# Turned score blocks in another layout, and the feed-forward part put under the list plan

## The chip, the core and the metric

The kernel runs on one core of a Trainium2 chip. The metric is device time in microseconds. TensorE (PE) multiplies, with its weight loads (PEld) beside it; VectorE (DVE) and ScalarE (ACT) do all elementwise work; SyncE (SP) issues nearly all DMAs.

## What is computed

Two batches of 3008 tokens. Attention without softmax, then two feed-forward networks (FFNs), all in float32:

```python
scores = scale * np.matmul(z, z.transpose(0, 2, 1))      # z: 2 x 3008 x 64
attn = np.maximum(scores, 0.0) ** 2
x = u * np.matmul(attn, v)                               # u, v: 2 x 3008 x 256
h = np.maximum(x @ moe_w_in, 0.0)                        # 256 -> 2048
x = h * h @ moe_w_out                                    # 2048 -> 256
h = x @ moe2_w_in
y = (h - np.tanh(h)) @ moe2_w_out
```

The weights come in float64, as pairs of 32-bit words.

## The kernel before

**Precision.** Each operand of a product is split into a high part (rounded to fp32r) and a low part, and each product is three matmuls: high by high, low by high, high by low. The splits are DVE and ACT work: an ACT copy or DVE cast makes the high part, a DVE subtraction the low part.

**Attention.** The queries of a batch are cut into six chunks (five of 512, the last of 448), so there are chunks 0 to 11. In each chunk 12 steps go over pairs of key blocks (256 keys). A step has scores (`scores`, L551, six matmuls of 64 rows), `relu` (L507) and `square` (L518) on ACT, `cast` to the high part (L487 on ACT or L489 on DVE), `low` (L496, DVE) and `values` (L588, 24 matmuls of 64 rows, two row groups at a time) that add into four PSUM banks. At the chunk's end `take` (L603 on ACT, L605 on DVE) evacuates the banks; the next chunk's values wait for it. `gate` (L610, DVE) multiplies with u for the first EARLY = 4 chunks, and `keep` stores x in DRAM; for the later chunks that product is made in the FFN part (`split_x`, L281).

**Mirrored steps.** The score matrix is symmetric. A pair of keys that lies in an earlier chunk is not computed again: `put` (L440) stores the squared block in DRAM, `get` (L446) loads it, `turn` (L456, or L462 twice in the last chunk of a batch) transposes its 32x32 blocks on DVE, and `cast` and `low` follow. In chunk t of a batch (t from 0 to 5) 2t of the 12 steps are mirrored: 60 in all. To make this fit, `keys` (L419) reads the keys of the first ten pairs in steps of four columns, `load_v` (L149) loads the rows of v in the same order, and relu writes runs of 128 (`views`, `wide`).

**Weights.** Each of the 32 weight units (16 a network, 512 KB after the split) costs nine operations in `split_w`: L240, L241, L244, L247 on the raw words, L250 and L253 on DVE, L242, L243 and L252 on ACT. 24 units are split during attention: STAY = 6 stay on chip, KEEP0 + KEEP1 = 18 are stored in DRAM and fetched at the end of attention. The last 8 are loaded and split in the FFN.

**Order.** In attention a planner writes the order of each engine: `attend` makes a Job for each operation with a cost, a due time (key), what it waits for and which buffers it takes and gives; `drive` plays them on a model of the engines (`ready`, `best`, `room`) and emits each in the order in which the model starts it. A turn costs 1.25 us there, or 1.4 (L1027). Weight units are due between step 10 and the start of chunk 5 in batch 0, and between step 76 and the start of chunk 11 in batch 1 (L954, L955). In the FFN the order is a fixed pattern: `front` (L643, six matmuls, then the elementwise work) runs LOOK = 3 steps ahead of `back` (L711, six matmuls); `interleave`, `pace`, `fill` and the lanes spread the weight and x splits between them. The steps of the first FFN (m1) run 21 steps ahead of those of the second (m2), one of each in turn.

Of the kernel before, what the change touches and what calls it, by code (L numbers as in the profile page):

```python
# [24 lines left out]
MARGIN = 6  # L25
READY = 3
# [17 lines left out]
def kernel(  # L44
# [221 lines left out]
    def load_x(c):  # L266
# [7 lines left out]
        return x, u

    def split_x(c, raw):
        n = chunks[c][2]
# [9 lines left out]
    class Lane:  # L287

        def __init__(self, units, ahead, width):
            self.todo, self.loaded, self.active = deque(units), deque(), deque()
            self.ahead, self.width = ahead, width

        def load(self, n, ready):
            need, _, load, split, args, nops = self.todo.popleft()
            self.loaded.append((need, ready, split, args, load(*args), nops))  # L300

        def refill(self, n, due):
            while (
                self.todo
                and len(self.loaded) + len(self.active) < self.ahead
                and self.todo[0][1] <= n
            ):
                self.load(n, n + READY)
            while self.loaded and len(self.active) < self.width:
                need, ready, split, args, raw, _ = self.loaded[0]  # L310
                if need > n if due else ready > n:
                    return
                self.loaded.popleft()
                self.active.append((need, deque(split(*args, raw)), n))

        def head(self):
            return min((u[0] for q in (self.active, self.loaded) for u in q), default=1 << 30)

        def pop(self, n, due, kinds):

            self.refill(n, due)
            if due:
                assert self.active or self.loaded or not self.todo or self.todo[0][0] > n
            for unit in self.active:


                if unit[0] <= n if due else unit[2] <= n and unit[1][0][0] in kinds:
# [870 lines left out]
```

## Time and profile before

| what | value |
|---|---|
| median of 3 runs (lowest to highest) | 1500.78 us (1499.35 to 1501.24) |
| profiled execution | 1500.66 us |
| its span | 1498.8 us |
| PE busy | 1481.7 us (99%), 8512 matmuls |
| DVE busy | 1262.8 us (84%) |
| ACT busy | 1048.9 us (70%) |
| mean granted clock of PE | 0.998 |

The span runs from the first instruction to the last. Busy matmuls reach into the time behind them, so a full PE row doesn't say that PE runs at its full rate; matmuls counted over a stretch do. Attention's first value matmul starts at 8.69 us, the FFN's first matmul at 467.01 us.

### The profile page before, as it was taken

Reading aid. Unit: us, or ns where it says so; the run is one execution under the profiler, and the core shown is the slowest. Engines: PE = TensorE matmul, PEld = TensorE weight load, DVE = VectorE, ACT = ScalarE, POOL = GpSimd, SP = SyncE. Lnnn points to the kernel's source line nnn. Section 1 sums busy time; section 2 is a strip of 40 time slices with the busy share of each in tenths; the row PEclk is TensorE's granted clock in tenths of the full one; section 3 lists DMA queues with packets and bytes.
Section 4 is the critical chain, followed back from the end, with each engine's and each line's share of the span. In section 5 each row is a group of like instructions: output and inputs, shape, how many; then the busy total and the mean of one; then the engine's idle time right before and its main releaser. Section 6 shows DMA issues by size and latency. Waiting matters only on the chain.

```text
span 1498.8 us, 22087 instructions
## 1 busy us (share of the span) xinstructions
PE 1481.7 (99%) x8512; PEld 1252.5 (84%) x8512; DVE 1262.8 (84%) x1907; ACT 1048.9 (70%) x1662; POOL 0.3 (0%) x6
## 2 busy tenths in 40 slices
PE   9999999999999999999999999999999999999999
PEld 7898878888878888888888888888888888888888
DVE  7899999888996899778788888878778787878788
ACT  8987558887654777667666666667666666766688
POOL 0000000000000000000000000000000000000000
PEclk9999999999999999999999999999999999999999
DMA  8857656777757200101001010101001010000000
GB/s 244 273 189 274 215 190 200 262 250 238 250 209 258 95 29 0 43 1 39 1 1 42 1 42 1 42 1 40 2 1 43 0 39 1 15 0 1 15 1 27
DMA packets 71529, 134.06 MB, mean 89 GB/s; under 512 B 4992, under 2 KB 47360, under 8 KB 67584
## 3 DMA queue, kind: packets, MB, share of 16 engines
q1 hardware_dynamic: 71120, 132.29, 25.9%
q8 instruction: 66, 1.08, 0.3%
q10 hardware_dynamic: 304, 0.38, 0.1%
q14 instruction: 39, 0.32, 0.1%
HBM read 79.43 MB, written 53.22 MB: 89 GB/s over the span
## 4 chain that ended last, share of the span: by engine, by line
PE 84%; DVE 10%; DMA 2%; ACT 2%; issue 2%; SPq 0%; DVEq 0%; ACTq 0%
PE o L711 34%; PE s L643 34%; PE o L588 14%; DVE at L456 3%; PE s L551 3%; DVE l L496 2%; DVE at L462 2%; ACT h L487 1%; DMA wraw<-in_moe_w_out_dram 1%; DMA zraw<-in_z_dram 1%; DMA wd<-wk 0%; DVE e L605 0%; DMA ww<-wd 0%; DVE wk L253 0%; DMA vraw<-in_v_dram 0%
## 5 line engine op out<-in xcount | busy, mean ns | idle before, releaser
L711 PE MATMUL o<-h,ww 128*128 128x512 f32 (+1 forms) x2304 | 576.2, 385 | 0.2 <-DVE h L658 0.2
L643 PE MATMUL s<-xs,ww 128*128 128x512 f32 (+1 forms) x2304 | 575.2, 385 | 0.0
L711 PEld LDWEIGHTS o<-h,ww 128*128 128x128 f32 x2304 | 432.4, 188 | 82.3 <-DVE h L658 0.7
L643 PEld LDWEIGHTS s<-xs,ww 128*128 128x128 f32 x2304 | 432.5, 188 | 81.1 <-issue 0.3
L588 PE MATMUL o<-h,vw 64*128 64x512 f32 (+1 forms) x2256 | 380.4, 387 | 5.2 <-DVE e L605 2.8
L588 PEld LDWEIGHTS o<-h,vw 64*128 64x128 f32 x2256 | 280.9, 186 | 44.1 <-DVE e L605 6.3
L588 PE MATMUL o<-l,vw 64*128 64x512 f32 (+1 forms) x1128 | 296.5, 387 | 6.9 <-DVE l L496 6.8
L658 DVE TENSOR_TENSOR h<-a,h 128x512 fp32r<-128x512 f32 (+1 forms) x192 | 130.7, 681 | 123.7 <-ACT h L656 122.7
L651 ACT ACTIVATE a<-s 128x512 f32<-128x512 f32 (+1 forms) x192 | 113.0, 589 | 173.2 <-PE s L643 171.4
L670 ACT ACTIVATE f<-s 128x512 f32<-128x512 f32 (+1 forms) x192 | 114.8, 598 | 125.9 <-PE s L643 125.9
L588 PEld LDWEIGHTS o<-l,vw 64*128 64x128 f32 x1128 | 172.1, 186 | 29.4 <-DVE l L496 10.9
L673 DVE TENSOR_TENSOR a<-s,a 128x512 f32<-128x512 f32 (+1 forms) x192 | 130.3, 678 | 32.9 <-ACT a L671 21.4
L689 DVE COPY_PREDICATED a<-small,f 128x512 f32<-128x512 uint8 (+1 forms) x171 | 127.3, 744 | 5.5
L487 ACT ACTIVATE h<-at 128x1024 fp32r<-128x1024 f32 (+1 forms) x60 | 61.5, 1024 | 93.2 <-DVE at L456 36.4
L652 ACT ACTIVATE a<-a 128x512 f32<-128x512 f32 (+1 forms) x192 | 119.7, 623 | 6.1
L692 DVE TENSOR_TENSOR h<-a,h 128x512 fp32r<-128x512 f32 (+1 forms) x172 | 117.9, 685 | 5.9
L686 DVE TENSOR_TENSOR f<-s,f 128x512 f32<-128x512 f32 (+1 forms) x171 | 117.2, 685 | 5.8
L672 ACT ACTIVATE f<-f 128x512 f32<-128x512 f32 (+1 forms) x192 | 121.7, 634 | 0.0
L671 ACT ACTIVATE a<-s 128x512 f32<-128x512 f32 (+1 forms) x192 | 113.9, 593 | 0.0
L656 ACT ACTIVATE h<-a 128x512 fp32r<-128x512 f32 (+1 forms) x171 | 106.4, 622 | 5.5
L496 DVE TENSOR_TENSOR l<-a,h 128x1024 fp32r<-128x1024 f32 (+1 forms) x83 | 100.2, 1208 | 10.4 <-ACT h L487 10.0
L518 ACT ACTIVATE a<-a 128x1024 f32<-128x1024 f32 (+1 forms) x83 | 87.1, 1052 | 1.2
(63 smaller groups left out, 1081.5 us busy)
## 6 DMA issues: line engine op xcount, KB each, us to landing
ad<-a SPq DMA_DIRECT2D x60, 512.0 KB, 4.2
m<-ad SPq DMA_DIRECT2D x30, 1024.0 KB, 6.5
wd<-wk SPq DMA_DIRECT2D x18, 512.0 KB, 3.0
ww<-wd SPq DMA_DIRECT2D x18, 512.0 KB, 7.7
wraw<-in_moe_w_in_dram SPq DMA_DIRECT2D x32, 256.0 KB, 4.8
wraw<-in_moe_w_out_dram SPq DMA_DIRECT2D x32, 256.0 KB, 4.9
vraw<-in_v_dram SPq DMA_DIRECT2D x22, 256.0 KB, 4.0
xr<-xd SPq DMA_DIRECT2D x10, 512.0 KB, 3.4
```

What stands on the lines that cost most here:

```text
L496: V.tensor_sub(l_, a_, h_)
L588: T.matmul(o[r * KD + d][:, :n], lhsT=w[halves[r], hl, g * D + d * P : g * D + (d + 1) * P], rhs=mv[halves[r], g, :n], start=x == 0 and (r ...
L643: T.matmul(s_, lhsT=w[:, hl, kd * P : (kd + 1) * P], rhs=mv[:, kd, :n], start=j == 0, stop=j == len(seq) - 1,)
L652: A.activation(a_, a_, AF.Square)
L658: main.append(lambda: V.tensor_sub(l[:, :n], a_, h[:, :n]))
L670: A.activation(f_, s_, AF.Tanh, scale=TB)
L672: A.activation(f_, f_, AF.Square, scale=TC)
L673: main = [lambda: V.tensor_sub(a_, s_, a_)]
L686: main.append(lambda: V.tensor_mul(g_, s_, f_))
L689: late.append(lambda: V.copy_predicated(a_, mask, g_))
L692: late.append(lambda: V.tensor_sub(l[:, :n], a_, h[:, :n]))
L711: T.matmul(o[d][:, :n], lhsT=w[:, side, (KD + d) * P : (KD + d + 1) * P], rhs=mv, start=k == 0 and j == 0, stop=k == NF - 1 and j == len(t ...
```

## The change

- `turn` is one DVE transpose for every chunk; it reads runs of 32 elements and writes in steps of four elements (16 bytes). The blocks in `put` and `get` keep their DMAs, but relu, cast, low and the opening now walk the score tiles in runs of 32 (`wide`, `views`, `cut`).
- `keys` and `load_v` take natural blocks of 128 keys and rows for every pair; still one DMA loads a pair of v blocks.
- The FFN's steps become Jobs of the same planner (`forward`); `front` and `back` keep their matmuls, and their elementwise work falls apart into `bend`, `power`, `shape`, `shape2`, `differ`, `mask`, `times`, `pick`, `high` and `rest`. `high` may go to ACT or DVE. The lanes and the fixed pattern are gone.
- m1 runs 41 steps ahead of m2, and this shrinks to 21 between m2's steps 32 and 160.
- 16 units are split in attention in place of 24 (KEEP0 + KEEP1 = 10); they are due one chunk earlier. The other 16 are split in the FFN.
- EARLY is 1: the product with u moves into the FFN for chunks 1 to 3.
- The planner counts buffers anew (w, h, raw, a, small, f, o), lets raw loads and h tiles take a free w buffer, counts two DMA issues for loads that send two, and looks only 60 us ahead.

The core of the diff:

```diff
-STAY, KEEP0, KEEP1 = 6, 6, 12
+STAY, KEEP0, KEEP1 = 6, 2, 8
 LANES = 8
-EARLY = 4
+AHEAD = 60.0
+EARLY = 1
...
-    lead = NF + LAG
+    lead = 2 * NF + LAG + 4
     steps += m1[:lead]
+    given = lead
     for i in range(len(m2)):
         steps.append(m2[i])
-        if lead + i < len(m1):
-            steps.append(m1[lead + i])
+        ahead = lead - (NF + 4) * min(max(i - 2 * NF, 0), 8 * NF) // (8 * NF)
+        while given < min(len(m1), i + 1 + ahead):
+            steps.append(m1[given])
+            given += 1
...
-            if j < 2 * (NC - 1):
-                rows = v[b, j // 2 * NMAX : (j // 2 + 1) * NMAX, :]
-                rows = rows.rearrange("(p t k) d -> t p k d", p=P, t=2)[j % 2]
-            else:
-                rows = v[b, 2 * j * P : 2 * (j + 1) * P, :].rearrange("(k p) d -> p k d", p=P)
+            rows = v[b, 2 * j * P : 2 * (j + 1) * P, :].rearrange("(k p) d -> p k d", p=P)
...
-        if p < 2 * (NC - 1):
-            return z.rearrange("r (p t k) -> r t k p", t=2, k=2)[:, p % 2, g]
...
-        if c % NC < NC - 1:
-            V.transpose(
-                a.rearrange("p g (j k) -> p k g j", k=16),
-                m.rearrange("p k (i t g) -> t p k g i", t=2, g=2)[p % 2],
-            )
-        else:
-            for g in range(2):
-                V.transpose(
-                    a[:, g].rearrange("p (s j m) -> p m s j", s=4, m=4),
-                    m.rearrange("p (m s) (i t g) -> t g p m s i", m=4, t=2, g=2)[p % 2, g],
-                )
+        V.transpose(
+            a.rearrange("p g (k j m) -> p m k g j", k=4, m=4),
+            m.rearrange("p (m k) (t g i) -> t p m k g i", m=4, t=2, g=2)[p % 2],
+        )
 
     def wide(x):
-        return x.rearrange("p (a x) -> p a x", a=4)
+        return x.rearrange("p (k a i) -> p k a i", k=4, a=4)
...
-            a.rearrange("p a g x -> p g a x"),
-            *(y.rearrange("p g (a x) -> p g a x", a=4) for y in tiles),
+            a.rearrange("p a g (k i) -> p g k a i", k=4),
+            *(y.rearrange("p g (k a i) -> p g k a i", k=4, a=4) for y in tiles),
...
+    def cut(a, g):
+        return a[:, :, g].rearrange("p a (k i) -> p k a i", k=4)
 
...
+        s = got[i] = single["s"].tile([P, NMAX], F32, tag="s", name="s")
...
+    def bend(i, func):
+
+        n = chunks[steps[i][1]][2]
+        a = sq[i] = ap_.tile([P, NMAX], F32, tag="a", name="a")[:, :n]
+        A.activation(a, got[i][:, :n], func)
+
+    def power(i):
+        A.activation(sq[i], sq[i], AF.Square)
...
+    def high(i, e, pool):
+
+        n = chunks[steps[i][1]][2]
+        pair[i] = pool.tile([P, 2, NMAX], F32R, tag="h" if pool is hp else "w", name="h")[:, :, :n]
+        if e == "A":
+            A.activation(pair[i][:, 0], sq[i], AF.Copy)
+        else:
+            V.tensor_copy(pair[i][:, 0], sq[i])
+
+    def rest(i):
+        V.tensor_sub(pair[i][:, 1], sq[i], pair[i][:, 0])
...
-        "w": [0.0] * (NW - 6),
-        "h": [0.0, 3.0],
+        "w": [0.0] * (NW - 6) + [4.0, 8.0],
+        "h": [0.0],
...
+    spare = {"h": 0, "raw": 2}
+    owed = [0]
...
+    def choices(pool):
+
+        if pool in spare and len(room["w"]) > owed[0] + spare[pool]:
+            times = room["w"][: len(room["w"]) - owed[0] - spare[pool]]
+            return sorted(room[pool] + times)
+        return room[pool]
...
+            if found and job.key > max(reached[0], found[0][1].key) + AHEAD:
+                break
...
+        ahead = at["m1", 0, 0]
+        for n in range(ahead, len(steps)):
+            until = min(n + (LOOK if n < end else FAR), len(steps) - 1)
+            while ahead <= until:
+                order_p.append(("f", ahead))
+                ahead += 1
+            order_p.append(("b", n))
...
+            hi = (b + 1) * nv - 2 * NV
+            if k < split:
+                step = lo + (k - first + 1) * (hi - lo) // count
+                need, asks = when["o", step], max(step - 12, 6)
+            else:
+                t0, t1 = when["f", at["m1", 0, 0]], when["f", at["m2", 0, 0]]
+                need = t0 + 6.0 + (k - split + 1) * (t1 - t0 + 10.0) / (2 * NF - split)
+                need, asks = min(need, when["f", at["m2", 0, f]] - 4.0), at["att", NCH - 1, 0] + 10
...
+                wjob[m, f] = Job(
+                    bring,
+                    when["f", at["m1", 0, f]] - 12.0,
+                    [(last + min(kept + 2, NV - 1), 0.0), (stages[-1], 0.0)],
+                    ["w"],
+                    S=2.6,
+                )
...
+            X = [("A", 1.06), ("V", 0.69), ("V", 0.69)]
+            give = [(2, xs_)]
+            if c >= EARLY:
+                X = [("V", 1.23), *X]
+                give = [(3, xs_), (0, us_)]
+                after.append((Job(ask2, need - 16.0, [(asks, 0.0)], ["raw"], [us_], S=2.6), 0.0))
...
+    def forward(kind, c, k, when, size, wjob, whold, xjob, xhold):
+
+        i = at[kind, c, k]
+        m, f = int(kind == "m2"), size(i)
+        alone = i > at["m1", NCH - 1, NF - 1]
+        need = when["b", i]
+        part = 1.36 if f == 1 else 1.22
+        s_, a, t_, small, hs = hold("f"), hold("a"), hold("t"), hold("z" if alone else "small"), hold(None)
+        after = [(wjob[m, k], 0.0), *xjob[m, c]]
+        if i == at["m1", 0, 0]:
+            after.append((("relu", NCH - 1), 0.0))
+        go = Job(lambda e, pools: front(i), when["f", i], after, ["f"], [xhold[m, c]], P=part)
+        go.name = ("f", i, 0)
+        A6, A63, V42, V69 = 0.6 * f, 0.63 * f, 0.42 * f, 0.69 * f
+        if m == 0:
+            one = Job(lambda e, pools: bend(i, AF.Relu), need - 3.2, [(go, 0.0)], ["a"], [s_], A=A6)
+            one = Job(lambda e, pools: power(i), need - 2.5, [(one, 0.0)], (), (), A=A63)
...
+        hi = Job(
+            lambda e, pools: high(i, e, homes[pools[0]]), need - 1.8, [(one, 0.0)], ["h"], [hs], A=A63, V=V42
+        )
+        lo = Job(lambda e, pools: rest(i), need - 0.8, [(hi, 0.0)], (), [a], V=V69)
+        give = [hs] + ([whold[m, k]] if c == NCH - 1 else [])
+        after = [(hi, 0.0), (lo, -0.8)]
+        come = Job(lambda e, pools: back(i), need, after, ["o", "o"] if k == 0 else (), give, P=part)
+        come.name = ("b", i, 0)
+        done[i] = come
...
-        ahead = at["m1", 0, 0]
-        for n in range(ahead, len(steps)):
-
-            until = n + (LOOK if n < end else FAR)
-            while ahead <= min(until, len(steps) - 1):
-                i, ahead = ahead, ahead + 1
-                due(i)
-                front(i)
-            while until >= len(steps) and late:
-                late.popleft()()
-            back(n)
```

## Rows read from the trace of the kernel before

**Rows 1.** Windows: us, busy PE, PEld, DVE, ACT, POOL (count), PEclk, DMA, GB/s.
```profile
50.32:89.59 39.27, 39.27 (x344) 35.36 (x343) 35.82 (x45) 35.29 (x43) 0.00 (x0) 1.00 0.65 216
89.59:126.58 36.99, 36.99 (x327) 33.31 (x325) 34.67 (x37) 29.70 (x35) 0.00 (x0) 1.00 0.70 239
126.58:164.59 38.01, 37.13 (x321) 31.07 (x318) 36.12 (x38) 24.92 (x29) 0.00 (x0) 1.00 0.60 212
164.59:203.74 39.15, 37.19 (x300) 30.52 (x301) 39.05 (x41) 23.54 (x28) 0.00 (x0) 0.96 0.62 215
203.74:243.43 39.69, 35.48 (x314) 32.15 (x313) 37.08 (x42) 24.25 (x32) 0.00 (x0) 0.96 0.50 167
...
359.58:396.90 37.32, 36.86 (x321) 30.15 (x318) 35.68 (x38) 26.80 (x32) 0.00 (x0) 1.00 0.61 208
396.90:433.72 36.82, 34.83 (x301) 28.59 (x301) 36.35 (x37) 20.70 (x25) 0.00 (x0) 1.00 0.63 219
433.72:467.01 33.29, 30.73 (x289) 26.79 (x289) 30.93 (x33) 15.28 (x18) 0.00 (x0) 1.00 0.69 253
467.01:515.96 48.95, 48.72 (x215) 40.00 (x214) 31.83 (x64) 31.14 (x53) 0.00 (x0) 1.00 0.58 203
515.96:1000.00 484.04, 484.04 (x2167) 406.56 (x2167) 398.60 (x682) 329.04 (x579) 0.00 (x0) 1.00 0.05 19
```

**Rows 2.** Chain of work in time order (start, us): a 448-wide step.
```profile
237.27 2.43 PE o L588 x24
```

**Rows 3.** Waits of PE (total, times, longest us).
```profile
PE o L588 <- DVE l L496: 6.8, 8, 2.2
PE o L588 <- DVE e L605: 2.8, 5, 1.0
```

**Rows 4.** Timeline, all engines, at the longest wait of PE (start, us).
```profile
224.49 2.20 DVE L462 STREAM_TRANSPOSE at<-m 128x512 f32<-128x512 f32 x2
...
226.53 1.09 DVE L496 TENSOR_TENSOR l<-at,h 128x896 fp32r<-128x896 f32 x1
...
227.68 0.47 PE L588 MATMUL o<-l,vw 64*128 64x448 f32 x2 [2.23 <-DVE l L496]
```

**Rows 5.** Lines by form, attention: count, busy us, mean ns, idle before.
```profile
L496 DVE TENSOR_TENSOR l<-a,h 128x1024 fp32r<-128x1024 f32 x76 | 92.3, 1214 | 10.4 <-ACT h L487 10.0
L456 DVE STREAM_TRANSPOSE at<-m 128x1024 f32<-128x1024 f32 x40 | 82.1, 2052 | 0.0
...
L496 DVE TENSOR_TENSOR l<-at,h 128x1024 fp32r<-128x1024 f32 x40 | 48.6, 1214 | 5.5 <-ACT h L487 4.2
...
L462 DVE STREAM_TRANSPOSE at<-m 128x512 f32<-128x512 f32 x40 | 42.1, 1120 | 0.0
...
L489 DVE CAST h<-a 128x1024 fp32r<-128x1024 f32 x34 | 23.5, 690 | 8.0 <-ACT a L518 5.4 <-PE o L588 1.9
```

**Rows 6.** Source view of L551, weight loads: ns min/median/max.
```profile
L551 PEld LDWEIGHTS s<-z x504: 184/305/334, 4.9 to 448.3; 64*128 64x128 f32 x168
```

**Rows 7.** Windows of the raw words (tile wraw): us, DVE busy (count), PEclk, DMA, GB/s.
```profile
164.59:203.74 39.15, 5.47 (x10) 0.96 0.62 215
...
467.01:515.96 48.95, 8.36 (x17) 1.00 0.58 203
```

**Rows 8.** Lines, the whole span: three operations of a weight unit.
```profile
L243 ACT ACTIVATE exp<-exp,ebias 128x512 int32<-128x512 int32 x32 | 22.8, 712 | 2.4 <-DVE exp L241 2.4
L250 DVE TENSOR_TENSOR mant<-mant,exp 128x512 f32<-128x512 f32 x32 | 21.9, 685 | 0.3
...
L242 ACT ACTIVATE mant<-mant 128x512 f32<-128x512 uint32 x32 | 19.9, 621 | 6.0 <-DVE mant L240 5.9
```

**Rows 9.** Timeline of PE in chunk 6: a strided score and the values before it.
```profile
252.39 0.62 PE L588 MATMUL o<-h,vw 64*128 64x512 f32 x4
...
253.07 0.87 PE L551 MATMUL s<-z 64*128 64x512 f32 x6
253.78 0.63 PE L588 MATMUL o<-h,vw 64*128 64x512 f32 x4
```

More of the change, by code (lines that the diff above doesn't have):

```diff
@@ L284, in split_x @@
             yield "V", lambda k=k: V.tensor_sub(xl[:, k, :n], x[:, k, :n], xh[:, k, :n])
[L287 to L327, printed above, removed]
-                    break
-            else:
-                return None
-            self.active.remove(unit)
-            engine, op = unit[1].popleft()
-            if unit[1]:
-                behind = unit[1][0][0] != engine and (engine == "A" or n >= at["m1", 0, 0])
-                self.active.append((unit[0], unit[1], n + 1 if behind else n))
-            return op
@@ L338 @@
-    x_units, k_units = [], []
     order = [(m, f) for m in range(2) for f in range(NF)]
     keeps = {STAY + k: k for k in range(KEEP0 + KEEP1)}
-    fetches = deque()
     split = STAY + KEEP0 + KEEP1
-    end = at["att", NCH - 1, 0]
-    for i, k in enumerate(range(STAY, len(order))):
-        m, f = order[k]
-        start = at["m1", 0, 0] + 2
-        if k < split:
-            fetches.append((start, m, f, keeps[k]))
-        else:
-            spare = -1 if k % 2 and k < len(order) - 2 else None
-            k_units.append((at[("m1", "m2")[m], 0, f], start, load_w, split_w, (m, f, spare), 9))
@@ new lines, in mask, with times @@
+            A.activation(small, fs[i], AF.Relu, scale=-1.0, bias=lbias)
+            least[i] = small.bitcast(U32)
+        else:
+            small = least[i] = mp.tile([P, NMAX], U8, tag="small", name="small")[:, :n]
+            V.tensor_scalar(small, fs[i], limit, None, op0=ALU.is_lt)
+    def times(i, alone):
+        n = chunks[steps[i][1]][2]
+        f = fs[i]
+        if alone:
+            gs[i] = tp.tile([P, NMAX], F32, tag="t", name="g")[:, :n]
+        V.tensor_mul(gs[i], got[i][:, :n], f)
@@ new lines, in back, with between, out @@
+                start=k == 0 and j % 3 == 0,
+                stop=k == NF - 1 and j % 3 == 2,
+            )
+    def between(c, d, e):
+        n = chunks[c][2]
+        if d == 0 and e == "A":
+            new_xs(1, c)
+        xh, xl = xs[1, c]
+        o = acc["m1", c][d][:, :n]
+        if e == "A":
+            A.activation(xh[:, d, :n], o, AF.Copy)
+        else:
+            V.tensor_sub(xl[:, d, :n], o, xh[:, d, :n])
+    def out(c, d, e):
+        n = chunks[c][2]
+        if d == 0:
+            xt["y", c] = xp.tile([P, KD, NMAX], F32, tag="x", name="y")
+        y, o = xt["y", c][:, d, :n], acc["m2", c][d][:, :n]
+        if e == "A":
+            A.activation(y, o, AF.Copy)
+        else:
+            V.tensor_copy(y, o)
@@ L967, in plan @@
+            raws = hold(None)
+            load = Job(ask, need - 12.0, [(asks, 0.0)], ["raw"], [raws], sends=2, S=2.8)
+            fresh = kept is None or kept < 2
+            owed[0] += fresh
             after = [(load, 0.0)]
[L968 removed]
+            if not fresh:
                 after.append((stages[kept - 2], 0.0))
[L970 to L971 removed]
+            give = [(5, raws), (6, hold("t")), (8, hold("t"))]
@@ L972, in plan, with begin @@
+            made = unit(W, split_w, (m, f, kept), raw)
+            def begin(k, made=made, fresh=fresh):
+                if k == 0:
+                    owed[0] -= fresh
+                made(k)
+            jobs = chain(W, need, after, ["t", "t"] + ["w"] * fresh, give, begin)
+            wjob[m, f] = jobs[-1]
             if kept is not None:
@@ L988, in plan @@
+        for kind in ("m1", "m2"):
+            for c in range(NCH):
+                for k in range(NF):
+                    forward(kind, c, k, when, size, wjob, whold, xjob, xhold)
         by = {}
```

409 lines of the change are left out of this document (196 added, 213 removed).

## The prediction

> **What bounds the kernel now.** I read the page first: TensorE (PE) is busy 99% of the span, so at most a few per cent are to be had, and the question is where it does less than its full rate. Next I cut the span at the first value matmul of each attention chunk [rows 1] (chunk c is the window that starts with it; six chunks a batch, the last of each batch 448 wide) and divided time by matmuls. The reader is to see two kinds of chunk. In chunk 2, 327 matmuls take 36.99 us, 0.113 us each, in chunk 1 it is 0.114: PE's own rate (a pair of row groups shares a slot). In the late chunks of both batches the same matmuls take longer. At 0.1135 us, chunk 3 (321) should take 36.4 us and takes 38.0; chunk 4 (300) 34.1 against 39.15; chunk 9 (321) 36.4 against 37.3; chunk 10 (301) 34.2 against 36.8. In the 448-wide chunks 24 matmuls take 2.43 us [rows 2], so 282 value matmuls take 28.55 us; with 32 wide ones (3.6 us) chunk 5 should take 32.2 us and takes 39.7, and chunk 11 with 7 should take 29.4 and takes 33.3. Lost: 1.6 + 5.1 + 7.5 + 0.9 + 2.6 + 3.9 = 21.6 us. (The share of busy time hides most of it: a busy matmul reaches far into the gap behind it, and in chunks 4 and 5 the mean granted clock is 0.96, that is, after idle stretches PE ran for a while at 1.2 GHz instead of 2.4.)
>
> Who is late there: the waits name VectorE's l (the low half, L496), then the evacuation at a chunk's turn (L605) [rows 3]. In those chunks VectorE (DVE) is busy 95, 99.7, 93, 96, 99 and 93% [rows 1], and at the longest wait, 2.2 us before 227.68, DVE is in two transposes and then the l that PE wants, with no idle time before them [rows 4]. So the late attention chunks are bound by DVE, and everything else by PE. The feed-forward part (FFN) loses nothing: from 516 to 1000 us PE is busy 100% with DVE at 82% and ScalarE (ACT) at 68% [rows 1]. What can be won is therefore about 21.6 us in attention; what can be lost is the 1030 us of FFN that now run without a stall.
>
> **The transposes.** 60 turns a run: 40 as one instruction of 2.05 us, 20 as two that together take 42.1/20 = 2.10 us [rows 5]. Per element that is 2.0 ns, against 1.2 ns of a subtraction of the same 1024 elements (1.214 us) [rows 5]. The new form reads runs of 32 and writes steps of 16 bytes. No row shows it. From below: a cast of 1024 elements takes 0.69 us [rows 5]; from above: nothing changes, 2.05. I take 1.21, the subtraction, for two reasons: both old forms read in steps of 16 bytes, one writes in steps of 64 bytes and the other of 16, and their price per element is the same, so it is rather the reading that costs; and PE's weight loads of the keys, which read in steps of 16 bytes in 60 of 84 scores, take 0.305 us (median) where the natural ones take 0.184 (minimum) [rows 6]. Gain: 0.84 us a turn (0.89 in chunks 5 and 11), 60 turns, some 51 us of DVE; of it 6, 8 and 10 turns lie in chunks 3, 4 and 5, and as many in 9, 10 and 11. The plan that orders attention already prices a turn at 1.25 us (L1027), so its order would also become true.
>
> The Trainium skill speaks against the half of this: SBUF — State Buffer, Specifications (TRN2), says that a line has 16 bytes and wants at least two hits for full bandwidth. The trace agrees for reads (2.0 against 1.2 ns); the page makes no difference between reading and writing, and the new writes still have one hit a line, so by it a turn would stay at 2.05 us. That is the first rival.
>
> **Weights that leave attention.** 24 units are split in attention now, 16 then (6 that stay, 10 stored and fetched in place of 18). A unit costs DVE 4 operations on the raw words, 0.51 us in the mean (13.83 us for 27 in two windows [rows 7]), and 0.69 + 0.69 for L250 and the last subtraction, which I take as long [rows 8]: 3.4 us; ACT 0.71 + 0.62 + 0.62 [rows 8], the last again taken as its neighbour: 1.95 us. The queue of SP also loses 8 pairs of loads, 8 stores and 8 fetches, each 512 KB, out of attention, and the FFN gets the 8 pairs of loads. Batch 0's units now end at step 48, the start of chunk 4, instead of step 60; batch 1's at 120 instead of 132: chunk 4 loses its 10 raw-word operations [rows 7], 2.5 units, 8.5 us of DVE. EARLY 4 to 1 moves three gates of 1.2 us (a product of the size of L496's) from attention into the split of x in the FFN, each with its 512 KB load of u.
>
> **What DVE needs then.** Chunk 3: 36.1 - 5.0 - 1.2 = 29.9 in 36.4 us (82%); chunk 4: 39.05 - 6.7 - 8.5 - 1.2 = 22.7 in 34.1 (67%); chunk 5: 37.1 - 8.9 - 1.2 = 27.0 in 32.2 (84%); chunks 9, 10 and 11 (no gate): 30.7 in 36.4, at most 29.7 in 34.2 (its units go too), 22.0 in 29.4 (87% and less). Chunk 1 runs at full rate with DVE at 91% and ACT at 90%, chunk 2 with 94% [rows 1]. So nearly all of the 21.6 us should go. What is late next is the turn between chunks (evacuations, L605 [rows 3]), which stays: I keep 1.5 us, between 0 and 6.
>
> **Keys in natural blocks.** A score of strided keys takes 253.78 - 253.07 = 0.71 us, three slots of values 253.07 - 252.39 = 0.68 [rows 9]. 60 scores by 0.025 us: 1.5 us less on PE. The v rows of a pair come as 1 KB pieces instead of 2 KB, one DMA as before; they are asked for 12 us ahead, only the first pairs of the opening lie on the path: 0, between -0.5 and +1. Relu, square, cast and low now walk runs of 32 instead of 128 on one side. Rows show that runs of 128 cost as much as none (L496 on the strided tile as on the turned one, 1.214 both [rows 5]): 0; even 0.1 us on each would be hidden at the shares above.
>
> **The FFN under the list plan.** Same matmuls, same order of PE but for the lead: 41 steps of the first FFN ahead, shrinking to 21. From 467 to 516 us, 215 matmuls are 17.9 lead steps of 2.73 us, with 17 raw-word operations, 4.25 units [rows 1, 7]. Less those, a step costs DVE (31.8 - 14.5)/17.9 = 0.97 us and ACT (31.1 - 8.3)/17.9 = 1.27. 41 steps are 112 us; DVE gets 40 + 16 units (54) + 3 gates (4) = 98 us, 88%, ACT 52 + 31 = 83 us, 74%. Chunk 1 bears more. After that no unit is left, and the mix has less to do than 516 to 1000 shows. Each DVE or ACT operation now waits in a planned order instead of a fixed pattern; behind a wrong order queue the split halves that back's matmuls want, three fronts later. The plan's prices (0.6, 0.63, 0.69) are close to the rows for such operations [rows 8]. SP's queue gets the loads in plan order too; a send that waits for its y holds back the loads of x and u behind it, which are asked 16 us early. I take +1 us, between 0 and the rival below.
>
> **Sum.** It is made against the profiled execution, 1500.66 us (span 1498.8 and 1.9 around it; the median of the runs is 1500.78, so the two are one): 1500.7 - 21.6 + 1.5 - 1.5 + 1 = 1480.1; I forecast 1480.
>
> **Rivals.** (1) The turns stay at 2.05 us: the change does not do what it says, and only the units and gates are gone. Chunks 4 and 5 then need 29.4 + 35.9 = 65 us of DVE in 66.3, chunks 10 and 11 36.4 + 30.9 = 67 less the units that leave chunk 10, in 63.6, chunk 3 35 in 36.4; with transposes in bursts and a plan that prices them 0.8 us too low, some 9 of the 21.6 us stay: 1488 (1484 to 1492). For it: the writes, and that no row has such an instruction; against it: that the old forms cost the same with two writing steps. (2) The FFN's list order lets PE wait: per pair of steps (first and second FFN, four groups of six matmuls, some 5.4 us) a late low half costs PE a little, 192 times. At 0.05 us it eats 10 us: 1490; it decides the sign at 21.5/192 = 0.11 us a pair, and at 0.2 us gives 1480 + 38 = 1518, slower than before. Its place would be the three h buffers and the order on DVE. For it: today's fixed pattern has no loss that could be mended, and the lead fills all of the shared buffers (four x splits alive). Against it: DVE at 82% and ACT at 68% leave 0.9 us and more free in each pair, and the same planner holds chunk 1 at full rate at 91%. (3) The turns fall below 1.2 us or the opening gains as well: nothing waits for that; 1477.
>
> **Chances.** Forecast (1476 to 1485): 0.67. Rival 1: 0.12. Rival 2: 0.05 between 1485 and 1492, 0.03 from there to 1497.7, 0.03 from there to 1503.7, 0.06 above. Rival 3: 0.04. The range from 1475 to 1492 leaves out about 0.14; cut at 1485 it would leave out 0.3. A measurement tells about 0.2%, 3 us, from no change: faster 0.67 + 0.12 + 0.08 + 0.04 = 0.91, same 0.03, slower 0.06.
>
> **What would show it.** Right: transposes at about 1.2 us in one form; DVE under 90% in chunks 4, 5, 10 and 11 and these at 34, 32, 34 and 29 us; key loads all near 0.19 us; no wait of PE over 0.3 us in the FFN. Wrong: transposes at 2 us with l still what PE waits for (rival 1); FFN windows with PE under 100%, waiting for h or its low half (rival 2); a lead stretch where ACT or DVE is over 95%.

## The result and the profile after

| | before | after |
|---|---|---|
| median of the runs | 1500.5 us (1499.35 to 1501.24, 4 runs) | 1482.89 us (1480.53 to 1483.26, 4 runs) |
| profiled execution, its span | 1500.66, 1498.8 us | 1482.63, 1480.7 us |
| first matmul of the FFN | 467.01 us | 444.29 us |
| PE from there to the start of its last matmul | 1028.0 us | 1032.6 us |

The ratio is 0.988, with a 95% interval of 0.9863 to 0.9897. The forecast of 1480 us and its range of 1475 to 1492 hold. Attention is 22.7 us shorter, the FFN 4.6 us longer, and 22.7 - 4.6 = 18.1 us is the difference of the spans. But the first thing to look at is a term of the sum that did not come true. From the groups of lines of the kernel after (count, busy us, mean ns, idle before):

```profile
L328 DVE STREAM_TRANSPOSE at<-m 128x1024 f32<-128x1024 f32 x60 | 121.8, 2031 | 0.0
```

The transpose, in one form as it was meant, still takes 2.03 us. Against 82.1 + 42.1 us in [rows 5] that is 2.4 us of VectorE less in all, not 51. The windows by chunk (columns as in [rows 1]; chunks 2 to 5, 9 to 11, then the FFN):

```profile
88.42:125.14 36.72, 36.72 (x327) 32.50 (x324) 33.81 (x38) 28.76 (x34) 0.00 (x0) 1.00 0.55 187
125.14:161.76 36.62, 36.33 (x320) 29.72 (x318) 34.05 (x34) 26.24 (x30) 0.00 (x0) 1.00 0.63 209
161.76:195.69 33.93, 33.93 (x302) 28.13 (x300) 31.70 (x23) 19.46 (x21) 0.00 (x0) 1.00 0.49 179
195.69:228.27 32.58, 32.54 (x315) 29.88 (x314) 31.59 (x31) 24.32 (x32) 0.00 (x0) 1.00 0.57 191
...
343.49:380.00 36.51, 36.33 (x320) 29.71 (x318) 33.40 (x32) 26.43 (x30) 0.00 (x0) 1.00 0.62 211
380.00:413.93 33.93, 33.93 (x302) 28.14 (x300) 31.71 (x23) 19.46 (x21) 0.00 (x0) 1.00 0.49 177
413.93:444.29 30.36, 30.33 (x292) 26.91 (x289) 26.38 (x22) 14.74 (x18) 0.00 (x0) 1.00 0.77 295
444.29:493.24 48.95, 48.41 (x213) 39.80 (x213) 34.93 (x62) 39.67 (x69) 0.00 (x0) 1.00 0.30 96
493.23:560.00 66.77, 66.77 (x297) 55.28 (x296) 54.09 (x98) 55.08 (x99) 0.00 (x0) 1.00 0.31 96
560.00:1000.00 440.00, 440.00 (x1969) 369.35 (x1968) 359.75 (x605) 309.39 (x550) 0.00 (x0) 1.00 0.06 19
...
1430.00:1480.70 50.70, 44.66 (x208) 39.77 (x206) 42.14 (x77) 40.25 (x83) 0.00 (x0) 0.95 0.06 20
```

The reader is to see that chunks 4 and 5 now take 33.93 and 32.58 us against 39.15 and 39.69 [rows 1], chunks 10 and 11 33.93 and 30.36 against 36.82 and 33.29, and that VectorE is still busy there to 93, 97, 93 and 87%: close to full, and yet PE loses next to nothing, and in chunks 4 and 5 its granted clock is 1.00 (2.4 GHz all through) where it was 0.96. Why the shares can be so high is in the windows of the turns alone (tile m; chunks 3, 4 and 5: us, VectorE busy and count, PEclk, DMA, GB/s):

```profile
125.14:161.76 36.62, 12.19 (x6) 1.00 0.63 209
161.76:195.69 33.93, 18.19 (x9) 1.00 0.49 179
195.69:228.27 32.58, 14.28 (x7) 1.00 0.57 191
```

8 and 10 turns belong to chunks 4 and 5; 9 and 7 are done in them, so VectorE works ahead. (Before does so too, but less: 16.49 and 17.30 us of turns there, some 8 in each chunk.) What the page of after says of PE's waits, and its weight loads of the keys (ns min/median/max):

```profile
PE o L583 <- DVE h L569: 3.1, 3, 1.8
...
PE o L457 <- DVE e L474: 0.5, 2, 0.3
PE o L457 <- DVE l L362: 0.4, 1, 0.4
```

```profile
L420 PEld LDWEIGHTS s<-z x504: 182/184/186, 4.9 to 427.0; 64*128 64x128 f32 x168
```

The low half (L362, once L496) is down from 6.8 us to 0.4 and the turn of chunks (L474) from 2.8 to 0.5 [rows 3]. The longest wait now lies in the FFN, at its very end (PE, then VectorE, from two timelines):

```profile
1466.36 2.19 PE L583 MATMUL o<-h,ww 128*128 128x448 f32 x10
...
1470.33 1.48 PE L583 MATMUL o<-h,ww 128*128 128x448 f32 x6 [1.78 <-DVE h L569]
...
1472.63 4.63 PE L583 MATMUL o<-h,ww 128*128 128x448 f32 x14 [0.82 <-DVE h L569]
```

```profile
1464.49 0.38 DVE L566 CAST h<-a 128x448 fp32r<-128x448 f32 x1
...
1466.40 0.39 DVE L566 CAST h<-a 128x448 fp32r<-128x448 f32 x1
```

Before, PE went through the last 30 matmuls of the FFN without a stop:

```profile
1488.59 6.77 PE L711 MATMUL o<-h,ww 128*128 128x448 f32 x30
```

After, its last 14 matmuls, behind the waits of 1.78 and 0.82 us, also run at a lower granted clock: 0.64 in the mean from 1472.63 to 1477.30 us, that is, in part at 1.2 GHz. They take 4.63 us where 14 of the 30 above take 3.16.

### The profile page after: what moved, and what is told of

It reads as the page before. It is cut to its first block, busy times and chain, and to the rows that moved or that the text cites. A ratio compares the mean times of both kernels' runs of the same rounds, so it can differ in the third digit from the quotient of the medians.

```text
span 1480.7 us, 21979 instructions
## 1 busy us (share of the span) xinstructions
PE 1471.2 (99%) x8512; PEld 1238.0 (84%) x8512; DVE 1232.4 (83%) x1830; ACT 1079.4 (73%) x1719; POOL 0.3 (0%) x6
## 4 chain that ended last, share of the span: by engine, by line
PE 96%; DVE 2%; DMA 1%; ACT 1%; issue 0%; SPq 0%; DVEq 0%; ACTq 0%
PE s L506 35%; PE o L583 34%; PE o L457 24%; PE s L420 3%; DVE at L328 0%; DVE l L362 0%; DMA vraw<-in_v_dram 0%; DMA zraw<-in_z_dram 0%; SPq L179 0%; ACT a L373 0%; ACT a L384 0%; SPq L159 0%; DVE e L474 0%; DVE a L557 0%; DVE a L535 0%
## 5 line engine op out<-in xcount | busy, mean ns | idle before, releaser
L457 PE MATMUL o<-h,vw 64*128 64x512 f32 (+1 forms) x2256 | 384.6, 383 | 0.7 <-DVE e L474 0.5
L457 PEld LDWEIGHTS o<-h,vw 64*128 64x128 f32 x2256 | 304.6, 184 | 40.8 <-DVE e L474 2.9
L457 PE MATMUL o<-l,vw 64*128 64x512 f32 (+1 forms) x1128 | 324.7, 383 | 0.4 <-DVE l L362 0.4
L569 DVE TENSOR_TENSOR h<-a,h 128x512 fp32r<-128x512 f32 (+1 forms) x384 | 249.6, 676 | 34.2 <-ACT h L564 31.0
L535 DVE TENSOR_TENSOR a<-s,a 128x512 f32<-128x512 f32 (+1 forms) x192 | 130.3, 679 | 107.3 <-ACT a L518 106.3
L457 PEld LDWEIGHTS o<-l,vw 64*128 64x128 f32 x1128 | 197.8, 184 | 20.2 <-DVE l L362 1.3
L564 ACT ACTIVATE h<-a 128x512 fp32r<-128x512 f32 (+1 forms) x244 | 149.8, 622 | 18.5 <-PE o L583 7.9
L557 DVE COPY_PREDICATED a<-small,f 128x512 f32<-128x512 uint8 (+1 forms) x171 | 127.2, 744 | 4.9
L328 DVE STREAM_TRANSPOSE at<-m 128x1024 f32<-128x1024 f32 x60 | 121.8, 2031 | 0.0
L554 DVE TENSOR_TENSOR f<-s,f 128x512 f32<-128x512 f32 (+1 forms) x171 | 117.0, 684 | 5.4
L362 DVE TENSOR_TENSOR l<-a,h 128x1024 fp32r<-128x1024 f32 (+1 forms) x83 | 100.7, 1214 | 16.8 <-ACT h L353 16.3
L353 ACT ACTIVATE h<-at 128x1024 fp32r<-128x1024 f32 (+1 forms) x60 | 61.5, 1024 | 71.7 <-PE o L457 58.2
L420 PE MATMUL s<-z 64*128 64x512 f32 (+1 forms) x504 | 85.1, 386 | 0.6 <-ACT a L395 0.6
```

Source lines behind the costliest of these rows:

```text
L328: V.transpose(a.rearrange("p g (k j m) -> p m k g j", k=4, m=4), m.rearrange("p (m k) (t g i) -> t p m k g i", m=4, t=2, g=2)[p % 2],)
L420: T.matmul(both[g], lhsT=keys(zt[b, p // 2][rows, hk, :], p, g), rhs=zt[b, q // NMAX][rows, hq, :n], start=t == 0, stop=t == 2,)
L457: T.matmul(o[r * KD + d][:, :n], lhsT=w[halves[r], hl, g * D + d * P : g * D + (d + 1) * P], rhs=mv[halves[r], g, :n], start=x == 0 and (r ...
L535: V.tensor_sub(sq[i], got[i][:, :n], sq[i])
L557: V.copy_predicated(sq[i], least[i], gs[i])
L564: A.activation(pair[i][:, 0], sq[i], AF.Copy)
```

## The experiments

**Theories.** L, for load: a late chunk takes what VectorE has to do in it (turns, low halves, the share of the weights), until that falls under PE's own time; whatever takes work off VectorE there brings its own part of the gain. The rivals: the plan's wrong price of a turn (1.25 us) was what made PE wait; or room: new buffer counts let VectorE run ahead, and the work itself counts for little. For the FFN: the list plan carries 16 units by itself, or only with the longer lead.

**1. The price of a step of 16 bytes** (`steps`). Nothing of the computation is left in; VectorE repeats fifteen operations of 1024 elements, among them both forms of the turn.

```diff
+V.transpose(runs(dst, 4), runs(src, 4))    # no step
+V.transpose(step(dst, 2), runs(src, 2))    # write 8 bytes apart
+V.transpose(step(dst, 4), runs(src, 4))    # write 16 bytes apart
+V.transpose(runs(dst, 4), step(src, 4))    # read 16 bytes apart
+V.transpose(step(dst, 4), step(src, 4))    # both
```

> A kernel of its own that leaves out the whole computation and runs, eight times each, DVE transposes, subtractions and copies of 1024 elements with rows read and written in runs or in steps. Theory 'one access a 16-byte line costs on either side': runs to runs 1.2 us, 8-byte steps on either side 1.2, 16-byte steps on the writing side alone 2.0, on the reading side alone 2.0, on both 2.0. Theory 'only reading costs' (that of the prediction): writing steps of 16 bytes 1.2, reading steps 2.0. Theory 'a transpose takes 2 ns an element whatever it walks': all nine 2.0. The subtraction and the copy with a step of 16 bytes on one side tell whether it is the transpose or the access: by the first theory both go up from 1.2 and 0.7 on either side.

Lines of VectorE (count, busy us, mean ns, idle before): L49 is the new turn, L52 the old one, L53 has no step, L54, L55 and L56 write 8, 16 and 64 bytes apart, L57 reads 8 and L58 16 bytes apart, L59 both writes and reads 16 bytes apart; L60, L61 and L62 are a subtraction without a step, writing and reading 16 bytes apart.

```profile
L59 DVE STREAM_TRANSPOSE a<-m 128x1024 f32<-128x1024 f32 x8 | 16.5, 2060 | 0.3
L52 DVE STREAM_TRANSPOSE a<-m 128x1024 f32<-128x1024 f32 x8 | 16.2, 2030 | 0.3
L49 DVE STREAM_TRANSPOSE a<-m 128x1024 f32<-128x1024 f32 x8 | 15.9, 1982 | 0.3
L58 DVE STREAM_TRANSPOSE a<-m 128x1024 f32<-128x1024 f32 x8 | 15.9, 1982 | 0.3
L55 DVE STREAM_TRANSPOSE a<-m 128x1024 f32<-128x1024 f32 x8 | 15.8, 1979 | 0.3
L61 DVE TENSOR_TENSOR a<-m 128x1024 f32<-128x1024 f32 x8 | 15.8, 1973 | 0.3
L62 DVE TENSOR_TENSOR a<-m 128x1024 f32<-128x1024 f32 x8 | 15.7, 1969 | 0.3
L56 DVE STREAM_TRANSPOSE a<-m 128x1024 f32<-128x1024 f32 x8 | 15.1, 1893 | 0.3
L54 DVE STREAM_TRANSPOSE a<-m 128x1024 f32<-128x1024 f32 x8 | 10.0, 1246 | 0.3
L53 DVE STREAM_TRANSPOSE a<-m 128x1024 f32<-128x1024 f32 x8 | 10.0, 1245 | 0.3
L57 DVE STREAM_TRANSPOSE a<-m 128x1024 f32<-128x1024 f32 x8 | 10.0, 1245 | 0.3
L60 DVE TENSOR_TENSOR a<-m 128x1024 f32<-128x1024 f32 x8 | 9.8, 1225 | 0.3
```

A step of 16 bytes costs 0.73 to 0.75 us on either side, a step of 64 bytes 0.65 (tried on the writing side alone), a step of 8 nothing, and the two sides don't add: 2.06 with both. That is the first of the three theories. The step of 16 bytes that the change took off the reading it put on the writing.

**2 to 4. One part of the change alone, in the kernel before.** The number of weights in attention (`before_units`), two of the buffer counts (`before_room`; the other counts stay), the layout of turns, keys and v (`before_layout`):

```diff
-STAY, KEEP0, KEEP1 = 6, 6, 12
+STAY, KEEP0, KEEP1 = 6, 2, 8
```

> The kernel before with 16 units in attention instead of 24 (KEEP0, KEEP1 = 2, 8), nothing else: turns stay at 2.05 us, due dates stay. Theory U (the units that left freed DVE): the six late chunks lose 6 to 10 us instead of 21.6, the FFN's first matmul comes at 452 to 456 us instead of 467; its fixed pattern must now split 16 units in a lead of 21 steps and may lose up to 15 us there, total 1487 to 1500. Theory P (the new planner's buffer accounting and horizon made the order better): the late chunks still lose 15 us or more, first FFN matmul at 461 or later.

```diff
-        "w": [0.0] * (NW - 6),
-        "h": [0.0, 3.0],
+        "w": [0.0] * (NW - 6) + [4.0, 8.0],
+        "h": [0.0],
```

> The kernel before with the changed kernel's count of free buffers in the plan (two more w buffers that come back from the opening, one h buffer where two were counted), nothing else. The run with 24 units in the changed kernel left 13 of the 23 us of attention to other things than the units. Theory P1 (the buffer count is most of these 13: DVE may run ahead of a busy chunk): first FFN matmul at 454 to 460 us instead of 467. Theory P2 (it is the layout, the gates or the rest of the planner): 463 to 468.

```diff
-            if j < 2 * (NC - 1):
-                rows = v[b, j // 2 * NMAX : (j // 2 + 1) * NMAX, :]
...
+        V.transpose(
+            a.rearrange("p g (k j m) -> p m k g j", k=4, m=4),
+            m.rearrange("p (m k) (t g i) -> t p m k g i", m=4, t=2, g=2)[p % 2],
+        )
```

> The kernel before with the layout alone: natural keys and v rows, one transpose a turn, score tiles in runs of 32; planner, units, gates and FFN as before. Natural keys give 1.5 us on PE, the single transpose 0.1 us of DVE a turn in chunks 5 and 11, that is 2 us. Theory P2a (layout is a small part): first FFN matmul at 462 to 466. Theory P2b (the layout is most of the 13 us): 454 to 459.

**5 and 6. The weights in the kernel after.** All 24 units in attention again, with the due dates of before (`after_24`); 16 units, with the due dates of before (`after_due`):

```diff
-STAY, KEEP0, KEEP1 = 6, 2, 8
+STAY, KEEP0, KEEP1 = 6, 6, 12
...
-            hi = (b + 1) * nv - 2 * NV
+            hi = (b + 1) * nv - NV
```

> The changed kernel with the units of before: 24 in attention (KEEP0, KEEP1 = 6, 12), due until the start of chunks 5 and 11. Theory U: the late chunks lose 8 to 18 us again, first FFN matmul at 452 to 461 us instead of 444.3, total 1488 to 1498. Theory P: first FFN matmul at 444 to 447, total 1480 to 1485.

> The changed kernel with the 16 units due as in the kernel before: until step 60 and step 132 in place of 48 and 120. If the due dates are part of what the units bring, the 2.5 units that chunks 4 and 10 then hold again cost VectorE 8.5 us there: its need rises from 31.7 to about 35 to 36 in chunk 4 (some of it taken over by turns made ahead), chunk 4 takes that instead of 33.93, and the first matmul of the feed-forward part comes 3 to 6 us after 444.29: total 1486 to 1489. If only the number of units counts (8 fewer, 27 us of VectorE over the attention part, with the turns made ahead as the buffer), it comes within 1 us of 444.29 and the total is 1482 to 1484.

| kernel | first FFN matmul, us | gain on 467.01 | total, us | ratio (95%) |
|---|---|---|---|---|
| weights alone | 463.14 | 3.9 | 1571.99 | 1.0486 (1.0470 to 1.0502) |
| room alone | 463.62 | 3.4 | 1497.91 | 0.9988 (0.9979 to 0.9998) |
| layout alone | 459.77 | 7.2 | 1493.31 | 0.9961 (0.9947 to 0.9975) |
| after, 24 units | 453.71 | 13.3 | 1491.90 | 0.9950 (0.9935 to 0.9965) |
| after, old due dates | 446.83 | 20.2 | 1484.43 | 0.9895 (0.9878 to 0.9911) |
| after | 444.29 | 22.7 | 1482.89 | 0.9880 (0.9863 to 0.9897) |

Chunk 4 in the windows of room, layout, weights, after with 24 units and after with the old due dates, in this order:

```profile
163.31:202.48 39.17, 36.56 (x301) 28.31 (x301) 39.08 (x41) 23.49 (x28) 0.00 (x0) 1.00 0.62 215
```

```profile
163.16:201.79 38.63, 36.26 (x301) 28.23 (x301) 38.50 (x40) 23.43 (x28) 0.00 (x0) 1.00 0.63 218
```

```profile
164.74:201.59 36.85, 36.45 (x301) 30.58 (x301) 35.94 (x34) 19.77 (x23) 0.00 (x0) 0.95 0.58 208
```

```profile
161.60:197.89 36.29, 34.92 (x304) 27.97 (x300) 35.66 (x36) 20.95 (x25) 0.00 (x0) 1.00 0.60 221
```

```profile
161.22:195.15 33.93, 33.93 (x302) 28.11 (x300) 33.85 (x32) 21.07 (x25) 0.00 (x0) 1.00 0.58 214
```

The reader is to see the first number beside the fourth: 39.17 against 39.08 of VectorE, 38.63 against 38.50, 36.85 against 35.94, 36.29 against 35.66; and at 33.85 and 31.70 the chunk stops at 33.93, PE's own time. Before has 39.15 against 39.05 [rows 1]. This is L, for chunk 4, over seven kernels with the turn at 2 us in all of them; chunk 10 shows the same (before 36.82 against 36.35, after with 24 units 36.27 against 35.64, at the old due dates 33.93 against 33.85). In chunks 5 and 11 the time falls with VectorE's work, but doesn't equal it: it lies 0.6 to 2.6 and 2.4 to 5.9 us above it. In chunk 11 of before PE waits 2.3 us for low halves, but also 1.4 us for an evacuation by ScalarE (L603).

The starts come from one profiled execution of each kernel, and executions of before alone run from 1498.2 to 1501.2 us: those with a mean clock of 1.000 take 1498.2 to 1499.4 us, the profiled one, at 0.96 in chunks 4 and 5, 1500.66. Room was profiled at 1.000, with 1.00 in chunk 4 although it takes as long as in before. So its 3.4 us are too many: by the ratio it brings 1.8 us (0.3 to 3.1). And the old due dates cost 2.5 us by the starts, 1.5 by the medians, with overlapping intervals. No part makes the gain alone: the three alone give 3.9 + 3.4 + 7.2 = 14.5 of 22.7 us, and the weights bring 9.4 us where the other parts are in (453.71 - 444.29), 2.5 of it by the due dates (446.83 - 444.29) and 6.9 by their number. The 13.3 - 7.2 - 3.4 = 2.7 us that remain, more with less for room, would fit the three gates (3 x 1.2 us); neither these nor the rest of the new planner were tried alone, so this is not shown.

Of the expectations, `after_24` came out by theory U and `before_room` by P2. `before_units` has its start by P, but its total of 1572 us is far outside the 1487 to 1500 us of U (P names none). `before_layout` (459.77) lies between its two theories, and so does `after_due`: chunk 4 stays at 33.93 us there, with 8 turns in place of 9, and the time is lost in chunk 5 (34.85 against 32.58 us) and chunk 11 (31.78 against 30.36).

Of the layout's 7.2 us the keys are 2.7: chunk 2, which nothing but PE bounds, falls from 36.99 [rows 1] to 36.72 us in each of the kernels with the new layout, 0.27 us for 6 strided scores, so 0.045 a score and 60 of these.

The weights alone also show what the old FFN makes of eight more units: it takes 1105.4 us in place of 1028.0, and most of that is PE waiting for them (PE's waits: total, times, longest us):

```profile
PE s L643 <- ACT ww L252: 49.0, 9, 5.7
```

**7. The price of a turn in the plan of before** (`before_price`).

```diff
-                    V=1.25 if f == 1 else 1.4,
+                    V=2.05 if f == 1 else 2.1,
```

> The kernel before with the turn priced at what it takes in the plan (2.05 and 2.1 us instead of 1.25 and 1.4), nothing else. If the false price made the order wrong and that cost the stalls: late chunks lose at most 12 us of 21.6, first FFN matmul at 457 or earlier, total about 1490. Theory U (DVE has too much to do there, in whatever order): they lose 17 to 23, first FFN matmul at 463 to 468, total 1497 to 1502.

1501.87 us, ratio 1.0017 (1.0007 to 1.0026); the FFN begins at 469.47, 2.5 us later than before, and chunk 4 takes 41.48 us. A true price doesn't help, so in the kernel before the false one was not what PE waited for.

**8. Less room after** (`after_w26`). The two w buffers that the change gives back after 4 and 8 us come at 430 us.

```diff
-        "w": [0.0] * (NW - 6) + [4.0, 8.0],
+        "w": [0.0] * (NW - 6) + [430.0, 430.0],
```

> The changed kernel whose plan gets the two w buffers back only at 430 us (the end of attention), so that attention is planned with 26 of them as before; nothing else. In the changed kernel chunk 4 runs 9 turns and chunk 5 only 7 (8 and 10 are due there): DVE works ahead. Theory R (running ahead needs the two buffers): chunks 4, 5, 10 and 11 lose 4 us or more again, first FFN matmul at 448 us or later. Theory L (the work taken off DVE is enough): first FFN matmul at 444 to 446.5 us, total 1482 to 1485.

1482.09 us, ratio 0.9883 (0.9868 to 0.9898), FFN from 444.27: no difference. With the load low enough VectorE runs ahead without them; room brought its 2 to 3 us only where VectorE was short.

**9. The lead of before, under the list plan** (`after_lead21`).

```diff
-    lead = 2 * NF + LAG + 4
+    lead = NF + LAG
...
-        ahead = lead - (NF + 4) * min(max(i - 2 * NF, 0), 8 * NF) // (8 * NF)
+        ahead = lead
```

> The changed kernel with the lead of before: 21 steps of the first FFN ahead instead of 41, list plan and 16 units in the FFN kept. Theory 'lead': 21 steps are 57 us and leave DVE some 37 us beside the first FFN's own work for 54 us of splits, so the second FFN waits for weights: 10 to 35 us lost in the first 150 us of the FFN, total 1492 to 1518. Theory 'list': the list order alone absorbs the 16 units, total 1481 to 1486. (With the fixed pattern and that lead, 16 units cost 77 us.)

1506.57 us, ratio 1.0046 (1.0031 to 1.0061). The FFN begins at 444.01 but takes 1056.9 us. Windows and the longest wait of PE:

```profile
444.01:493.00 48.99, 39.74 (x175) 32.59 (x174) 35.49 (x63) 39.09 (x68) 0.00 (x0) 0.96 0.33 107
493.00:560.00 67.00, 59.96 (x222) 45.79 (x223) 60.84 (x109) 49.90 (x87) 0.00 (x0) 0.88 0.29 95
```

```profile
PE s L506 <- ACT xs L272: 9.3, 1, 9.3
```

175 + 222 matmuls against 213 + 297 in the same time: the 113 that are missing, at 0.225 us each (66.77/297), are 25 us; PE's waits up to 600 us are 16.3 of them, and the clock of 0.96 and 0.88 goes with the rest. The second FFN, whose 16 units are split in this stretch, starts 20 steps sooner, and VectorE and ScalarE haven't done with the splits. (The longest wait is not for weights, as theory 'lead' had it, but for a split of x, L272, which shares the engines with them.) The lead of 41 carries the units, and the list plan alone doesn't.

**10 and 11. A turn without a step** (`after_24_fast`, `after_24_fast2`), with 24 units so that its effect could show. For this the block of the mirrored step must lie otherwise on chip, so its load is cut into 4 or 2 DMAs.

```diff
-        rows = ad[block].rearrange("a (j m) k x -> (a j) (m k x)", m=4)
-        SP.dma_start(out=m.rearrange("p k x -> p (k x)"), in_=rows)
+        for g in range(4):
+            rows = ad[block][:, g * 32 : (g + 1) * 32].rearrange("a j k x -> a j (k x)")
+            SP.dma_start(out=m[:, 4 * g : 4 * g + 4].rearrange("p k x -> p (k x)"), in_=rows)
...
-            a.rearrange("p g (k j m) -> p m k g j", k=4, m=4),
+            a.rearrange("p g (k m j) -> p m k g j", k=4, m=4),
```

> The changed kernel with 24 units in attention, due as before, and turns that read and write runs of 32: the load of a block fetches rows j, j+32, j+64, j+96 for a partition (four DMAs of 256 KB in 2 KB pieces instead of one of 1 MB in 8 KB pieces), so that no write is strided. By the single transposes measured alone a turn takes 1.25 us. Theory L (what bounds the late chunks is the sum of DVE work, whichever part of it is taken away): first FFN matmul at 443 to 447 us instead of 453.7, total 1480 to 1485. If the units matter by something else (their DMAs, their buffers): 450 to 454.

> The changed kernel with 24 units in attention, due as before (453.7 us to the first FFN matmul with the turn at 2.03 us), and a turn of two transposes of 512 elements that read runs of 32 and write steps of 8 bytes; a block is fetched by two DMAs of 512 KB in 4 KB pieces. The four pieces of the run before came late (DVE waited 93 us for them); two lanes a block instead of four should let them land in time. By the single transposes a turn takes 1.3 to 1.4 us. Theory L (the sum of DVE work bounds the late chunks): 38 us of DVE less, first FFN matmul at 443 to 447, total 1480 to 1485. If the loads are late again: over 455, with DVE waiting for m.

1612.51 and 1613.45 us, ratios 1.0755 (1.0739 to 1.0771) and 1.0760 (1.0744 to 1.0776). From the groups and VectorE's waits of the first, then of the second (two transposes of 512 elements a turn, writing 8 bytes apart):

```profile
L329 DVE STREAM_TRANSPOSE at<-m 128x1024 f32<-128x1024 f32 x60 | 74.2, 1239 | 95.6 <-DMA m<-ad 92.7
```

```profile
DVE at L329 <- DMA m<-ad: 92.7, 18, 10.5
```

```profile
L330 DVE STREAM_TRANSPOSE at<-m 128x512 f32<-128x512 f32 x120 | 80.1, 695 | 85.4 <-DMA m<-ad 83.6
```

```profile
DVE at L330 <- DMA m<-ad: 83.6, 28, 5.9
```

The turns do take 1.24 and 2 x 0.70 us, so the price that the prediction took exists, in another layout. But the loads of the blocks come late, up to 10.5 us at a time, and the kernel is bound by them. These two runs say nothing of L. SP's own record tells where the time goes: issuing one such load keeps it busy for 1.76 and 1.40 us (median; 120 and 60 loads), where issuing the whole block took 0.44 us (30 loads, in `after_24`). In the first run SP does nothing but issue seven of them in the 16.69 us from 198.96 us on, and eight in the 19.19 us from 218.15 us on. Why an issue takes so long, by the shape of the reads or by what is already in the queue, stays open.

**12. The tail** (`after_tail`). In the steps where only the second FFN is left, the high part stays on ScalarE.

```diff
-    [(one, 0.0)], ["h"], [hs], A=A63, V=V42
+    [(one, 0.0)], ["h"], [hs], **({"A": A63} if alone and i < len(steps) - 1 else {"A": A63, "V": V42})
```

> The changed kernel with the high parts of the last 20 steps (second FFN alone) on ACT only, as in the kernel before; nothing else. In the changed kernel DVE made five of those casts near the end and was late: PE lost about 4 us in the last 9 us (before: under 1). Theory T: PE's last matmul comes 3 to 4 us earlier, total 1478.5 to 1480. Rival: ACT, with five operations a step, becomes the late one: no gain or up to 3 us of loss, 1482 to 1486.

1480.25 us (1479.85 to 1480.81), ratio 0.9872 (0.9856 to 0.9889). The end of the FFN in the windows, and PE's waits there:

```profile
1430.00:1477.70 47.70, 42.90 (x207) 38.15 (x205) 41.15 (x73) 41.57 (x87) 0.00 (x0) 1.00 0.06 21
```

```profile
PE o L583 <- ACT h L564: 1.4, 2, 0.7
```

The FFN takes 1030.0 us in place of 1032.6, and the clock stays at 1.00 where it was 0.95. Theory T is a little short (2.6 us, not 3 to 4): PE still waits 1.4 us, now for ScalarE's cast (L564). This version is the best by its median, 2.6 us under the kernel after, though the intervals of the two ratios overlap, and the one execution of after with a mean clock of 1.000 took 1480.53 us, no more than this version: a good part of the gain may be that the clock no longer falls.

## Why the prediction was right, and where it was not

**What bounds the kernel: right.** Chunks 4 and 10 take what VectorE has to do, down to PE's own 33.93 us; experiments 2 to 6 show it. Chunks 5 and 11 follow it, with something more on top that the low halves don't explain by themselves.

**The transposes: wrong.** The step that failed is the price of 1.21 us, and in it the reason "it is rather the reading that costs". 60 turns gave VectorE 2.4 us, not 51. That both old forms cost the same, one writing 64 bytes apart and one 16, doesn't free the writing: they also read 16 bytes apart, and the two sides don't add. The only thing [rows 5] could say was that either side may cost it all, so the "agrees for reads" of the prediction wasn't to be had from them either. The Trainium skill (SBUF — State Buffer, Specifications (TRN2)) asks for at least two hits in each line of 16 bytes; with writes 16 bytes apart at 1.98 us and 8 bytes apart at 1.246, the trace agrees, for writes too.

**Rival 1: its condition came true, its time did not.** The turns stayed at 2.03 us, and rival 1 said 1488. Its own sum was nearly right: 65 us of VectorE in 66.3 for chunks 4 and 5; after shows 31.70 + 31.59 = 63.3 in 66.5. What failed is the surcharge, some 9 us for bursts and a false price. The price cost nothing in the kernel before (experiment 7), and the bursts did no harm here, VectorE working ahead: 9 and 7 turns in chunks 4 and 5 instead of 8 and 10. For chunk 4 the forecast need of 22.7 us, plus 8 turns that didn't get shorter (6.7) and the one done ahead (2.0), is 31.4; measured 31.70.

So the forecast holds for a smaller reason than it gave, and in part by luck: by the prediction's own sum the turns as they came out mean 1488 us. The weights, the gates, the room and a turn shorter by 0.02 to 0.07 us were together enough to get under PE's time. The 51 us weren't needed, but there was little to spare: with 24 units chunk 4 needs 35.66 us, and the FFN begins 9.4 us later (experiment 5). Of the signs named, the chunks' times came as forecast (34, 32, 34 and 29; measured 33.93, 32.58, 33.93 and 30.36); VectorE under 90% came in chunk 11 alone.

**The weights: right**, place and size: chunk 4 has no raw-word operation any more, and without its turns VectorE has 13.51 us to do there (31.70 - 18.19) in place of 22.56 (39.05 - 16.49): 9.05 us less, forecast 9.7 with the gate. And with the kernel otherwise as after the units decide 9.4 us.

**The keys: mis-sized.** The loads are at 0.184 us as forecast, but a score gained 0.045 us, not 0.025: 2.7 us, not 1.5. The estimate by one score against three slots of values [rows 9] was too coarse; two equal chunks at PE's rate would have been the better rows.

**What stays in attention: right.** 22.7 us are 2.7 for the keys, 0.4 for an earlier start (8.31 against 8.69 us) and, as what remains, 19.6 of the 21.6 us; 2.0 stay, where 1.5 were kept, about half of it in chunk 11 (30.36 us against the 29.4 of the prediction).

**The FFN: right in the lead, mis-sized in all.** 16 units, 3 gates and 41 steps fit: from 444 to 560 us VectorE is busy 77% and ScalarE 82% (forecast 88 and 74: together the same, with more of it on ScalarE), and PE loses 0.5 us in one place, at 484 us. But +1 us became +4.6, and "no wait over 0.3 us" is wrong. Rival 2 looked for the loss in every pair of steps; it lies at the end, where only the second FFN is left. A step there has two PE groups of 1.21 us, 2.43 in all, and VectorE's four operations of 448 elements (L535, L557, L554, L569) take 0.62 + 0.67 + 0.61 + 0.61 = 2.51 us, with the cast (0.38) 2.9: the plan gave VectorE the cast where it already had as much to do as PE. The 4.6 us add up: waits of 1.8 and 0.8 us at the end, 0.5 at 484 us, and 1.5 for the last 14 matmuls at the lower clock (4.63 against 3.16 us), a cost that the prediction had not listed. Experiment 12 takes 2.6 us back: the 1.5 of the clock, and the waits at the end fall from 2.6 to 1.4 us.

**The sum.** Forecast: 20.1 + 1.5 - 1 = 20.6 us; the spans show 19.6 + 0.4 + 2.7 - 4.6 = 18.1. Two errors of size with opposite signs, keys and FFN, and one wrong price that the late chunks didn't need.

## What to carry to other kernels

When two engines are close, work out for each stage the need of the slower one against the time of the other, and stop at the crossing: there a part of the change may fail and the time still come out. On VectorE in float32, moving a step of 16 bytes from the reading to the writing side saves nothing (1.982 against 1.979 us); measure the form alone before it is built into a layout. And where work leaves a full stage for another, ask what buffer of time receives it: eight more units cost 77 us in the old FFN (1105.4 against 1028.0), in the list plan with the old lead some 24 (1056.9 against 1032.6) more than with 41 steps of lead, where PE loses 0.5 us in that stretch.

## What the runs showed of the hardware that was not expected

A step of 16 bytes costs VectorE the same on the reading and on the writing side (1.98 us for a transpose of 1024 float32 a partition against 1.245 without; subtraction 1.97 against 1.225), both together hardly more (2.06), and a step of 8 bytes nothing (1.246). The load of a block of 1 MB, cut into 4 or 2 DMAs for a better layout, came so late that VectorE waited 93 and 84 us for it: each issue held SP for 1.76 and 1.40 us in place of 0.44, and why stays open. Two waits of 1.8 and 0.8 us at the end of the FFN were followed by a granted clock of 0.64 over the last 4.7 us (experiment 12, with waits of 0.7 and 0.7 us there, kept 1.00).
